# First attention of a fused attention and feed-forward kernel: the stride of the token order moved from a VectorE write to TensorE's transposes, and one row of weight rounding moved to the next stage

## The chip, the cores and the metric

The kernel runs on one core of a Trainium2 chip. The metric is the device time of one execution in microseconds. The kernel before took 1344.98 us (median of three runs, 1344.81 to 1346.94).

In the text PE is TensorE (PEld its weight loads), DVE is VectorE, ACT is ScalarE, POOL is GpSimd and SP is SyncE, whose queue issues nearly all transfers.

## What is computed

```python
# q, k, v: (8, 12, 448, 64) float32; g_q, g_k: (64,)
q_n, k_n = rmsnorm(q, g_q), rmsnorm(k, g_k)         # x / sqrt(mean(x*x) + 1e-6) * g, over the 64
scores = q_n @ k_n.T / sqrt(64)
attn = softmax(scores)                              # (448, 448) for each of 96 heads
attn_out = attn @ v
x = attn_out.transpose(0, 2, 1, 3).reshape(3584, 768)
h = x @ w_in                                        # (768, 2048), float64 weights
out = maximum(h, 0) ** 2 @ w_out                    # (2048, 768), float64 weights
```

## The kernel before

The eight batches are worked on in four spans of two batches. A span has an attention, a first product (`x @ w_in` and the squared ReLU) and a second product. Two heads make a pair, so that 128 partitions are filled, and a span has 12 pairs. The two products are done with seven smaller products each (named A11, S2, S1, S3, A12, A22, S4) in place of eight; this needs sums of weight blocks and of `x`.

Only the first span's attention runs with no product of an earlier span beside it: `attention_alone`. It and the first product after it, here called L1, are the stages that the change touches. On the trace the first runs until 133 us, L1 until about 262 us.

**The first attention.** A load of q puts four neighbouring tokens into one partition: partition p holds tokens 4p to 4p+3 (112 partitions). After the norm, `transpose(i, s, n)` turns each of the four chunks of q (s = 0) and of k (s = 1) with PE into a PSUM bank `pt` (L782), and ACT copies the bank to `qkT` (L784 for k, L786 for q with the gains). Chunk j has the tokens 4p+j, so the 448 columns of `qkT` stand in the order (j, p) and not in that of the tokens. Keys stand on partitions of the scores and may have any order, as long as v has the same. Queries are columns of the scores, of the values `pav` and of the sums `tot`, and stay in the order (j, p) until the end of the pair. There `finish(i)` makes the factors 1/sum with two DVE transposes and a reciprocal (L913 to L915), and multiplies (L922). This multiplication writes x in the order of tokens:

```python
            x = x.rearrange("d (p j) -> d j p", j=NJ)
            pav, factors = (t.rearrange("d (j p) -> d j p", j=NJ) for t in (pav, factors))
```

so that `pav` and `factors` are read one float after the other, and `xT` is written at every fourth float. `first_pair`, which runs ahead of the program's main part, has the same transposes for pair 0 (L380).

In a pair's turn stand, in this order: two score chunks and their exponentials (`scores`, L807 on PE, L811 on ACT), k's transposes for the next pair, the values' second half of the pair before (L870), the running sum of the exponentials (`add_up`, L824 on DVE), the norm's squares on ACT (L722) and their sums on DVE (L723, L724) for the pair after next, q's transposes for the next pair, the norm's root (`roots`, L733 to L738, on ACT, DVE and POOL), two more score chunks, the column sums `tot` (L895), the values' first half, and `finish` of the pair before. Each engine works through its own list in the order in which the code issues it; nothing is reordered by a scheduler.

**The rounding.** The weights come as float64, and are turned into float32 blocks on the chip in 32 rows, 16 of `w_in` and then 16 of `w_out`. `prepare(t)` is cut into four steps by its `yield`s; a row passes through a load of 768 KB (L540, L543), ACT (L589, L606), DVE (L603, L608, L613), and the sums of blocks on POOL (L583). For rows below `EARLY // 4` POOL also adds exponent and mantissa in two halves (`value`, L575); for later rows DVE does it in one instruction (L579). Every second row a store of seven blocks, 1344 KB, goes to DRAM (L598), from where PE's weights `sw` are read later (`load_blocks`, L672, five buffers). Loads, stores and `sw` are all in SP's queue.

How many steps stand beside which stage is set by two lines, one in the loop over `attention_alone` and one in that over L1 (u counts the turns; NAT is 12, N1 is 56, ALL is 140):

```python
    EARLY, ALL = 4 * 13, 4 * (2 * NFC + 3)
                weights(min(EARLY, 2 * u + 1, 4 + (EARLY - 4) * u // (4 * NAT - 7)))
                weights(min(ALL, EARLY + (ALL - EARLY) * (u - 1) // (N1 - 6)))
```

**L1.** For each of eight f there are seven groups of three matmul passes (L1098) against blocks `sw`; DVE adds their results (L1106, L1109, L1114), and ACT applies ReLU and square (L1066, L1068). The steps of the rounding stand between the groups.

Of the kernel before, what the change touches and what calls it, by code (L numbers as in the profile page):

```python
# [304 lines left out]
def places_of(qk, i, work):  # L305


    first, second = i % 2 * 4 + work, i % 2 * 4 + 2 + (i // 2 + work) % 2
    return qk[:, first:second + 1:second - first]


def load_q(nc, qk, q, i):

    _, H, S, D = q.shape
    b, h0 = divmod(2 * i, H)
    nc.sync.dma_start(places_of(qk, i, 0)[:S // 4, 0].rearrange("p (h e) -> p h e", h=2),
                      q[b, h0:h0 + 2].rearrange("h (p j) d -> p h (j d)", j=4))


def load_k(nc, qk, k, i):  # L320

    _, H, S, D = k.shape
    b, h0 = divmod(2 * i, H)
    dst = places_of(qk, i, 0)[:S // 4, 1].rearrange("p (j h d) -> p j h d", j=4, h=2)
    for h in range(2):
        nc.sync.dma_start(dst[:, :, h], k[b, h0 + h].rearrange("(p j) d -> p j d", j=4))


def normalise_in_turn(nc, raw, sq, rstd, mhalf, between=lambda: None):

    SP, _, n = rstd.shape
    for s in range(2):
        nc.scalar.activation(sq[:, s], raw[:, s], AF.Square)
        nc.vector.tensor_reduce(rstd[:, s], sq[:, s].rearrange("p (n d) -> p n d", n=n), AX, ALU.add)
        nc.vector.tensor_scalar(rstd[:, s], rstd[:, s], float(n) / sq.shape[2], 1e-6, ALU.mult, ALU.add)
        nc.gpsimd.tensor_tensor(rstd[:, s], rstd[:, s], mhalf[:SP, 0:n], ALU.pow)
        if s == 0:
            between()
            nc.vector.tensor_tensor(sq[:, 0].rearrange("p (j h d) -> p h j d", j=n // 2, h=2),
                                    raw[:, 0].rearrange("p (h j d) -> p h j d", j=n // 2, h=2),  # L340
                                    rstd[:, 0].rearrange("p (h j) -> p h j ()", h=2)
                                    .to_broadcast([SP, 2, n // 2, sq.shape[2] // n]), ALU.mult)


def first_pair(tc, q, k, g_q, g_k, held):

    nc = tc.nc
    qk, qkT, ident, mhalf, gains, rstd, bound = held
    D = q.shape[-1]
    S = q.shape[2]  # L350
    NJ = 4
    SP = S // NJ
    raw, sq = (places_of(qk, 0, n)[:SP] for n in range(2))
    load_q(nc, qk, q, 0)
    bound[0]()
    load_k(nc, qk, k, 0)
    for i, g in enumerate((g_q, g_k)):
        for h in range(2):
            nc.gpsimd.dma_start(gains[h * D:(h + 1) * D, i:i + 1], g.rearrange("(d o) -> d o", o=1))
    load_q(nc, qk, q, 1)  # L360
    load_k(nc, qk, k, 1)
    nc.gpsimd.memset(mhalf, -0.5)
    make_identity(nc, ident)


    def between():
        bound[1]()
        nc.vector.tensor_scalar(gains[:, 0:1], gains[:, 0:1], gains[:, 1:2], float(D) ** -0.5, ALU.mult, ALU.mult)

    with tc.tile_pool(name="ps_first", bufs=1, space=bass.MemoryType.PSUM) as ps_first:  # L370

        nc.vector.memset(qkT[:, 1], 0.0)
        idle = ps_first.tile([2 * D, S], F32, name="idle")
        for _ in range(3):
            nc.tensor.matmul(idle, qkT[:, 1, 0, 0:2 * D], qkT[:, 1, 1], start=True, stop=True)
        normalise_in_turn(nc, raw, sq, rstd, mhalf, between)
        for s, src in ((1, raw[:, 1]), (0, sq[:, 0])):
            pt = ps_first.tile([2 * D, S], F32, name=f"pt{s}")
            for j in range(NJ):
                nc.tensor.transpose(pt[:, j * SP:(j + 1) * SP], src[:, j * 2 * D:(j + 1) * 2 * D], ident[:SP, :SP])  # L380
            if s:
                nc.scalar.copy(qkT[:, 0, s], pt)
            else:
                nc.scalar.activation(qkT[:, 0, s], pt, AF.Copy, scale=gains[:, 0:1])
# [3 lines left out]
def attention_then_ffn_bounded(  # L388
# [35 lines left out]
    nc = tc.nc  # L424

    B, H, S, D = q.shape
    NT, DM = out.shape
    DFF = w_in.shape[1]
    P = 128
    NJ = 4  # L430
    SP = S // NJ
    NPAIR = H // 2
    NFC = DFF // P
# [26 lines left out]
    def bank(name, n=None):  # L460

        turn[0] += n is None
        return ps_m.tile([P, S], F32, tag="mn"[turn[0] % 2 if n is None else n], name=name)

    qk, qkT, ident, mhalf, gains, rstd0, _ = held
# [20 lines left out]
    HW = HC * P  # L486
    WORDS, BLOCKS, EXPS = 7, 2, 4

    EARLY, ALL = 4 * 13, 4 * (2 * NFC + 3)
    assert DM == NW and BLOCKS * 8 * HW + EXPS * NW + 2 * NW <= 3 * HF * S and 2 * NW <= 4 * S and HF % 4 == 0  # L490


# [184 lines left out]
    vs, probs, pavs, tots, normed, rstds = {}, {}, {}, {}, {}, {0: rstd0}  # L677
# [100 lines left out]
    def transpose(i, s, n):  # L778

        pt = bank("pt", n)  # L780
        for j in range(NJ):
            nc.tensor.transpose(pt[:, j * SP:(j + 1) * SP], normed[i][s][:, j * P:(j + 1) * P], ident[:SP, :SP])  # L782
        if s:
            nc.scalar.copy(qkT[:, i % 2, s], pt)  # L784
        else:
            nc.scalar.activation(qkT[:, i % 2, s], pt, AF.Copy, scale=gains[:, 0:1])  # L786
# [116 lines left out]
    def finish(i):  # L903

        b, hp = divmod(i, NPAIR)
        x = factors = xT[:, b % 2, hp]
        if i < NAT:
            pav = pavs.pop(i)


            turned, factors = sums["turned"], sums["factors"]
            few = small.tile([P, S // 32], F32, tag="few", name="few", bufs=1)
            nc.vector.transpose(turned, tots.pop(i))  # L913
            nc.vector.reciprocal(few, turned.rearrange("p (g r) -> p g r", r=32)[:, :, 0])
            nc.vector.transpose(factors.rearrange("p (g r) -> p g r", r=32),  # L915
                                few.rearrange("p g -> p g ()").to_broadcast([P, S // 32, 32]))

            x = x.rearrange("d (p j) -> d j p", j=NJ)
            pav, factors = (t.rearrange("d (j p) -> d j p", j=NJ) for t in (pav, factors))
        else:  # L920
            pav = rests.pop(i)
        nc.vector.tensor_tensor(x, pav, factors, ALU.mult)  # L922
        del vs[i]
# [15 lines left out]
    def attention_alone():  # L939


        for i in range(NAT):
# [5 lines left out]
            if i == 0:  # L948

                transpose(1, 1, 1)  # L950
                scores(0, 2)
                scores(0, 3)
                transpose(1, 0, 0)
                add_up(0, 1)
                norm(2)
                load_v(1)
                values(0, (0, 1))
                load(3)
                yield
                continue  # L960
            if more:
                transpose(i + 1, 1, 0)
# [16 lines left out]
            total_of(i - 1)  # L979
            values(i, (0, 1))  # L980
            finish(i - 1)
            yield
            if added(i) == 3:
# [5 lines left out]
        values(i, (2, 3))  # L989
        total_of(i)  # L990
        finish(i)
        combine_x(i)

    def attention(first):
# [3 lines left out]
        for i in range(first, last + 1):  # L998
# [42 lines left out]
            if i > first:  # L1041
                finish(i - 1)
                combine_x(i - 1)
# [511 lines left out]
def kernel(  # L1555
# [41 lines left out]
    with tc.manual_schedule():  # L1597

        nc.scalar.preload_act_table_set("natural_log_exp_and_others")
        first_pair(tc, q, k, g_q, g_k, held)  # L1600
# [4 lines left out]
    with tc.If(bits <= limit) as small_scores:  # L1605
        with tc.manual_schedule():
            attention_then_ffn_bounded(tc, *args, held)
# [32 lines left out]
```

## Time and profile before

| | before |
|---|---|
| median of three runs | 1344.98 us |
| the profiled execution | 1345.02 us |
| its span | 1343.1 us |
| granted PE clock | 0.998 |
| PE busy, share of the span | 1324.0 us, 99% |
| DVE busy | 860.5 us, 64% |
| ACT busy | 486.2 us, 36% |
| POOL busy | 681.1 us, 51% |
| first matmul of L1 starts at | 133.3 us |

Busy time of an engine is the time that its instructions took, and a share is an average over stages with different limits. A matmul's recorded time overlaps with the next one's, so a group of matmuls is read by its length from first start to last end. The difference of 1.9 us between the execution and its span lies around the program. In the answers below, "A <- B" after an idle time names the instruction that ended it.

### The profile page before, as it was taken

The numbers are of one execution on the slowest core, as the hardware profiler recorded it, in microseconds if no ns is written. First come the engines' busy times: TensorE is split into PE (matmuls) and PEld (weight loads), VectorE is DVE, ScalarE is ACT, GpSimd is POOL, SyncE is SP. The second block draws the span as 40 slices with busy tenths as digits, with TensorE's granted clock in tenths as the row PEclk, the third lists the DMA queues.
The fourth block names the chain that finished last, engine by engine and source line by source line (L and its number), as shares of the span: only waits on it lengthen the run. The fifth ranks groups of instructions, "written<-read, shape, count | busy, mean of one in ns | idle before, by whom it ended". The sixth has DMA issues, their size and how long they took to land.

```text
span 1343.1 us, 17769 instructions
## 1 busy us (share of the span) xinstructions
PE 1324.0 (99%) x5930; PEld 699.4 (52%) x5930; DVE 860.5 (64%) x1333; ACT 486.2 (36%) x939; POOL 681.1 (51%) x546
## 2 busy tenths in 40 slices
PE   8999999999999999999999999999999999999997
PEld 3333544444446655444444755444444665556887
DVE  6999888489988233467887523457878723336553
ACT  7886566455541012245543011235554101111000
POOL 5766534376765222647774522448676522322452
PEclk9999999999999999999999999999999999999999
DMA  8978899656664433356656432345664444431333
GB/s 225 240 221 218 289 372 307 213 124 132 133 148 119 102 88 88 97 116 125 145 127 144 109 91 88 95 114 115 134 130 124 120 92 143 128 88 47 115 104 55
DMA packets 413817, 190.18 MB, mean 142 GB/s; under 512 B 282388, under 2 KB 408724, under 8 KB 413716
## 3 DMA queue, kind: packets, MB, share of 16 engines
q1 hardware_dynamic: 406164, 180.21, 51.8%
q0 software_dynamic: 4736, 8.40, 2.4%
q8 instruction: 49, 0.80, 0.3%
q10 hardware_dynamic: 2816, 0.34, 0.2%
q14 instruction: 52, 0.43, 0.1%
HBM read 155.72 MB, written 33.16 MB: 141 GB/s over the span
## 4 chain that ended last, share of the span: by engine, by line
PE 86%; DVE 7%; ACT 3%; DMA 3%; issue 1%; POOL 0%; SPq 0%; DVEq 0%; ACTq 0%; POOLq 0%
PE ps L1198 21%; PE pd L1098 10%; PE pa L1098 10%; PE pc L1098 10%; PE sc L799 7%; PE pav L881 7%; PE pb L1098 5%; PE ps L1381 3%; PE ps L1249 2%; PE pd L1353 2%; PE pc L1353 2%; PE pa L1353 2%; PE pd L1183 1%; PE pc L1183 1%; DMA sw<-w1s 1%
## 5 line engine op out<-in xcount | busy, mean ns | idle before, releaser
L1070 POOL TENSOR_TENSOR gT<-gT 128x448 f32<-128x448 f32 x96 | 93.7, 978 | 258.5 <-ACT gT L1066 258.5
L764 POOL TENSOR_TENSOR half<-half,mhalf 128x28 f32<-128x28 f32 x36 | 185.2, 5145 | 69.5 <-DVE half L763 54.9
L1198 PE MATMUL ps<-gT,sw 128*128 128x448 f32 x432 | 169.3, 545 | 0.0
L1066 ACT ACTIVATE gT<-gT 128x448 f32<-128x448 f32 x96 | 55.4, 577 | 296.2 <-DVE gT L1114 296.2
L1098 PE MATMUL pa<-xT,sw 128*128 128x448 f32 x384 | 154.9, 539 | 0.5 <-DMA sw<-w1s 0.5
L1198 PEld LDWEIGHTS ps<-gT,sw 128*128 128x128 f32 x432 | 80.1, 190 | 87.2 <-issue 85.0
L1198 PE MATMUL ps<-gC,sw 128*128 128x448 f32 x288 | 113.1, 546 | 0.0
L799 PE MATMUL sc<-qkT 64*64 64x448 f32 (+1 forms) x1152 | 110.0, 496 | 0.3 <-ACT pr L801 0.2
L1098 PEld LDWEIGHTS pa<-xT,sw 128*128 128x128 f32 x384 | 72.8, 190 | 71.4 <-issue 71.4
L583 POOL TENSOR_TENSOR gC<-gC 128x384 f32<-128x384 f32 x64 | 76.3, 1209 | 60.2 <-DVE gC L579 58.5
L1114 DVE TENSOR_TENSOR gT<-z,pd 128x448 f32<-128x448 f32 x32 | 19.8, 620 | 102.2 <-PE pd L1098 102.2
L849 POOL DMA_DIRECT2D xT<-factors x72 | 38.0, 532 | 92.8 <-DMA factors<-square 65.7
L1198 PEld LDWEIGHTS ps<-gC,sw 128*128 128x128 f32 x288 | 53.2, 190 | 59.5 <-issue 58.3
L801 ACT ACTIVATE pr<-sc 128x896 f32<-128x896 f32 x87 | 76.9, 908 | 12.3 <-PE sc L799 12.1
L766 POOL TENSOR_TENSOR qk<-qk,half 128x448 f32<-128x448 f32 x72 | 77.1, 1092 | 2.8
L1098 PE MATMUL pd<-xT,sw 128*128 128x448 f32 x192 | 77.9, 542 | 0.2
L1098 PE MATMUL pc<-xT,sw 128*128 128x448 f32 x192 | 77.5, 540 | 0.2 <-DMA sw<-w1s 0.2
L1098 PE MATMUL pd<-xC,sw 128*128 128x448 f32 x192 | 77.4, 539 | 0.0
L1098 PE MATMUL pb<-xC,sw 128*128 128x448 f32 x192 | 77.4, 539 | 0.0
L1098 PE MATMUL pc<-xC,sw 128*128 128x448 f32 x192 | 77.4, 539 | 0.0
L881 PE MATMUL pav<-pr,vt 64*64 64x448 f32 x348 | 72.7, 537 | 0.0
L881 PE MATMUL rest<-pr,vt 64*64 64x448 f32 x348 | 72.7, 537 | 0.0
(282 smaller groups left out, 2453.1 us busy)
## 6 DMA issues: line engine op xcount, KB each, us to landing
sw<-w1s SPq DMA_DIRECT2D x224, 192.0 KB, 2.4
sw<-w2s SPq DMA_DIRECT2D x102, 256.0 KB, 3.4
w1s<-gC SPq DMA_DIRECT2D x8, 1344.0 KB, 6.4
w2s<-gC SPq DMA_DIRECT2D x8, 1344.0 KB, 6.8
qk<-in_q_dram SPq DMA_DIRECT2D x144, 56.0 KB, 2.6
qk<-in_k_dram SPq DMA_DIRECT2D x144, 56.0 KB, 2.4
xT<-factors POOLq DMA_DIRECT2D x72, 112.0 KB, 3.5
words<-in_moe_w_out_dram SPq DMA_DIRECT2D x9, 768.0 KB, 6.9
```

The costliest lines, as they stand in the source:

```text
L583: nc.gpsimd.tensor_tensor(*[blocks_of(n)[:, place_of(n, i)] for i in (dst, x, y)], op)
L764: nc.gpsimd.tensor_tensor(half, half, mhalf, ALU.pow)
L766: nc.gpsimd.tensor_tensor(qkn[:, s], raw[:, s], half[:, s * NG:(s + 1) * NG].rearrange("p g -> p g ()").to_broadcast([P, NG, 32]), ALU.mult)
L799: nc.tensor.matmul(sc[part, h, 0:n], qkT[rows, 0, 1, keys], qkT[rows, 0, 0, of], start=True, stop=True)
L801: nc.scalar.activation(pr, sc[:, :, 0:n], AF.Exp)
L881: nc.tensor.matmul(into, vs[i][rows, h, c, :], probs[i, c][rows, h, :], start=(c == 0), stop=(c == NF), skip_group_check=True)
L1066: nc.scalar.activation(g, src, AF.Relu)
L1070: nc.gpsimd.tensor_tensor(g, g, g, ALU.mult)
L1098: nc.tensor.matmul(ps, stream[n + at][:, c], rhs[:, c], start=first and c == 0, stop=c == HC - 1, skip_group_check=not first)
L1198: nc.tensor.matmul(ps, stream[n][:, c % 4], rhs_of[i][:, c], start=c == 0, stop=c == HF - 1)
L1353: nc.tensor.matmul(ps, lhs[:, c], rhs[:, c], start=first and c == 0, stop=c == HK - 1, skip_group_check=not first)
L1381: nc.tensor.matmul(ps, weights_of(o, m, c // HK)[:, c % HK], rhs_of[i][:, c, part], start=c == 0, stop=c == HF - 1)
```

## The change

Three things change, all in the first span. q's transposes (s = 0) write chunk j to the columns j, j+4, j+8 and so on of the bank, so that the columns come in the order of tokens from there on; k's transposes (s = 1) write as before. The multiplication in `finish` then reads and writes everything in that order, with no rearrangement. And `EARLY` is 48 in place of 52, so that twelve rows of the rounding lie beside the attention and twenty beside L1; row 12 is then one of those whose exponent and mantissa DVE adds.

```diff
+def chunk_of(pt, s, j, n):
+
+    return pt.rearrange("d (j p) -> d j p", j=n)[:, j] if s else pt.rearrange("d (p j) -> d j p", j=n)[:, j]
+
+
 def first_pair(tc, q, k, g_q, g_k, held):
...
-                nc.tensor.transpose(pt[:, j * SP:(j + 1) * SP], src[:, j * 2 * D:(j + 1) * 2 * D], ident[:SP, :SP])
+                nc.tensor.transpose(chunk_of(pt, s, j, NJ), src[:, j * 2 * D:(j + 1) * 2 * D], ident[:SP, :SP])
...
-    EARLY, ALL = 4 * 13, 4 * (2 * NFC + 3)
+    EARLY, ALL = 4 * 12, 4 * (2 * NFC + 3)
...
-            nc.tensor.transpose(pt[:, j * SP:(j + 1) * SP], normed[i][s][:, j * P:(j + 1) * P], ident[:SP, :SP])
+            nc.tensor.transpose(chunk_of(pt, s, j, NJ), normed[i][s][:, j * P:(j + 1) * P], ident[:SP, :SP])
...
-
-            x = x.rearrange("d (p j) -> d j p", j=NJ)
-            pav, factors = (t.rearrange("d (j p) -> d j p", j=NJ) for t in (pav, factors))
```

## The prediction

> **What bounds the kernel now.** I first asked where the time is made, with the windows view over the two stages that the change touches: the first attention, until 133 us, and the first product L1, until 262 us. The columns are the stretch, its length, busy time (and instructions) of PE, PEld, DVE, ACT and POOL, then clock, DMA share, GB/s.
>
> ```profile
> 31.00:107.00 76.00, 71.70 (x368) 27.31 (x370) 72.95 (x105) 61.83 (x112) 50.19 (x39) 1.00 0.81 231
> 107.00:133.00 26.00, 25.47 (x128) 9.76 (x124) 23.91 (x36) 17.95 (x34) 18.75 (x10) 1.00 0.88 216
> 133.00:240.00 107.00, 106.28 (x281) 53.06 (x281) 92.16 (x116) 60.32 (x93) 48.21 (x46) 1.00 0.93 324
> ```
>
> From 31 to 107 us PE (71.70 of 76) and DVE (72.95 of 76) are both nearly full; DVE is at 96%. In L1 PE is full, DVE is at 86%, the DMA engines at 93%. Which of the two ends last in the attention is told by the chain of work that ended last (start, length, what):
>
> ```profile
> 31.21 1.07 DVE gT L824
> 32.28 1.14 DVE rstd L723
> ...
> 37.89 0.66 DVE gT L915
> 38.57 1.03 DVE xT L922
> ...
> 40.31 1.89 DVE gT L824
> 42.20 1.14 DVE rstd L723
> ...
> 47.17 0.99 DVE xT L922
> ...
> 114.44 1.69 PE sc L807 x8
> ```
>
> It runs mostly through DVE until 107 us, with the multiplication of `finish` (L922) in it, and is PE alone from 114 us on. What PE loses by it is in its waits up to 265 us (total us, times, longest):
>
> ```profile
> PE pt L782 <- ACT qkT L784: 3.2, 7, 1.0
> PE sc L807 <- ACT gT L811: 2.2, 3, 1.0
> PE pa L1098 <- DMA sw<-w1s: 0.5, 1, 0.5
> ```
>
> ACT is only the messenger: in the same stretch its own longest wait is for DVE (L733 for the sums of L724: 13.9 us in 8 waits). So the attention can give back a few microseconds of PE's idle time, no more.
>
> [...] where every operand is contiguous and one is in PSUM (L1106: 618 ns), and L922, which writes every fourth float, takes 997 ns. [...] the trace's excess is (997-618)/448 = 0.85 ns an element. [...] Nothing in this trace has PE writing with a stride[...].
>
> ```profile
> L922 DVE TENSOR_TENSOR xT<-pav,gT 128x448 f32<-128x448 f32 x12 | 12.0, 997 | 0.4
> L1106 DVE TENSOR_TENSOR z<-p,pb 128x448 f32<-128x448 f32 x11 | 6.8, 618 | 19.9 <-PE pb L1098 18.4 <-ACT gC L589 1.4
> 38.39 0.60 PE L782 MATMUL pt<-ident,qk 112*128 112x112 f32 x4
> ```
>
> **The change, part by part.** (1) `finish`: 12 multiplications lose the stride. 12 x (0.997-0.618) = 4.5 us of DVE. Seven of them lie between 31 and 107 us, where DVE sets the pace: 2.7 us there. No wait is added or removed.
>
> (2) Row 12 of the rounding goes from the attention to L1. The attention runs 44 steps instead of 48 over the same 41 turns, so DVE loses one each of L603, L608 and L613 (0.8+0.95+0.95 = 2.7 us), ACT one L606 and one L589 (0.92 each, 1.8 us), POOL about two adds L575 (1.1 to 1.4 us each), and SP's queue one load of 768 KB and one store of 1344 KB. Spread evenly, 76/125 of DVE's 2.7 us, 1.6 us, falls between 31 and 107.
>
> Together DVE has 2.7 + 1.6 = 4.3 us less to do there: 68.7 us against PE's 71.7. DVE is then no longer the fuller engine, and PE is late next. What PE can win is its own slack: the idle stretches in its timeline from 31 to 107 us are 1.02, 0.80, 0.21, 0.43, 1.02, 0.17, 0.98 and 0.22, 4.9 us, and the three score runs behind such a gap last 2.05 instead of 1.76 us, 0.9 us more. So the gain lies between 0 and 5.8 us, and not above 4.3 where DVE is the cause, plus up to 0.5 us of gaps after 107. The chain also holds ACT's exponentials, POOL's scaling L738 and loads of k (one of 5.05 us at 57.4), which the change doesn't shorten. I take **3.5 us**, between 1.5 and 5.
>
> (3) q's 48 transposes write with a stride. Four take 0.60 us, of which the last one's own 0.26 us is latency: (0.60-0.26)/3 = 0.113 us from start to start. A 448-column matmul of L1 is issued every 2.25/6 = 0.375 us, 0.84 ns a column, so 112 columns at that rate take 94 ns: a transpose has about 20 ns to spare, and its pace is probably that of its weight load (140 ns of its own row, overlapping). [...] I take **no cost**, hidden under the weight load. If PSUM charges what SBUF charges (0.85 ns x 112 = 95 ns each), PE gets 48 x 0.095 = 4.6 us more, nearly all in a stage where PE is at 94%. A gain is excluded: nothing is taken away. ACT's copies L784 and L786 read `pt` as before.
>
> (4) L1 takes what the attention gives. DVE there: 2.7 us plus the add of row 12, which it now does itself (L579, 1.0 to 1.1 us): 3.8 us. DVE waits for PE's outputs in all about 26 us of L1's 129 us and so has room on average, but the steps come denser: 92 instead of 88 over the same 50 turns, 4.5% more. Where DVE is fullest (9.58 of 10 us from 180 to 190) it gets to 9.9, and PE's banks are freed later behind it; there before already one matmul group lasted 2.52 instead of 2.25 us. DMA: 2.1 MB more on 39.5 MB. From 150 to 210 us the engines are at share 1.0 and 365 to 404 GB/s; 2.1 MB at 375 GB/s are 5.6 us, of which the nearly idle start (136 GB/s from 130 to 140) takes a part. SP's queue carries rows, stores and the blocks `sw` in one order. A store waits for POOL's sums (L583; 6.9 us in 6 waits), and with it each `sw` behind it, for which PE waits:
>
> ```profile
> 217.68 8.72 DMA sw<-w1s
> 226.44 2.52 PE pc L1098 x6
> ...
> 232.16 6.18 DMA sw<-w1s
> 238.48 2.49 PE pa L1098 x6
> ```
>
> Five buffers of `sw` are 11.3 us of PE's work, landing takes 4.6 us in the middle and 8.7 at most; most of the addition is covered by that lead. I take **1.0 us** lost, between 0 and 3 (a block landing late by the whole 5.6 us less part of the lead).
>
> Sum: -3.5 + 0 + 1.0 = **-2.5 us**. The stages after 262 us keep their order and are PE's. The profiled execution took 1345.02 us (span 1343.1 and 1.9 around it), beside a median of 1344.98, so both give the same: **1342.5 us**.
>
> **The rivals.** *A: the strided write is dear* (slower). Its place is L782, its price from 0.095 us each upward. At 0.095, 4.6 us of PE eat the 3.5 gained: -3.5+4.6+1.0 = +2.1, 1347 us. At twice that, 0.19 us, 9.1-3.5+1.0 = +6.6: 1351.6. It decides from (3.5-1.0)/48 = 52 ns a transpose on (a spacing of 165 ns instead of 113), and is seen as slower from 5.2/48 = 108 ns. [...] against it the slow column rate of these float32 passes and the weight load beside them.
>
> *B: L1 gives all back.* DMA and DVE there are near full at once; a stall like those at 226 and 238 us, repeated in five or six places at 0.5 to 0.8 us, makes 3 to 4 us: 1345 to 1346. For it the share of 1.0, against it PE's total of less than 1 us of idle time there now.
>
> *C: everything is hidden in L1 and the attention reaches PE's pace:* -4 to -5 us, 1340.5. For it DVE's 4.3 us; against it the chain's other members.
>
> **How the numbers follow.** 0.2%, 2.7 us, is about what a measurement of this kernel can tell from no change. The likeliest case (0.55) runs from -4.5 to 0 with -2.5 in its middle: 0.30 faster, 0.25 same. C (0.10) is faster. B (0.15): 0.09 same, 0.06 slower. A (0.20): 0.06 same, 0.14 slower. Sums: faster 0.40, same 0.40, slower 0.20. The likeliest case alone spans 1340.5 to 1345. The range takes in most of C and of B, and A until somewhat under twice SBUF's price: 1339.8 to 1349.
>
> **What would show it.** Right: L922's successor near 620 ns; four transposes of q still 0.57 to 0.60 us; PE's waits at L782 and L807 down from 5.4 us to under 2.5; the first matmul of L1 at about 129.8 us instead of 133.3; L1 at 129 to 131 us, its waits for `sw` about 1 us. Wrong: four transposes of q lasting 0.9 us or more (A); the first L1 matmul earlier but L1's end not, with longer waits for `sw` or for DVE's reads of PSUM (B); DVE faster and PE's gaps unchanged, which would say that loads of k or ACT hold the chain.

## The result, and the profile after

The changed kernel takes **1341.43 us** (median of 13 runs, 1339.04 to 1344.22), the kernel before 1344.03 us (median of 13 runs on the same chip, 1343.54 to 1346.94). By the medians it is 2.6 us faster. The ratio, estimated over all these runs, is 0.9973, with a 95% interval from 0.9966 to 0.998: 3.6 us faster, between 2.7 and 4.6. The profiled execution took 1340.13 us (span 1338.3), which is 4.9 us less than the profiled one of before and 1.3 us under its own median; the executions after the change scatter over 5 us, those of before over 3.

The windows of the kernel after, with the columns as before. The first is the same stretch; the others end where L1 now begins and where the profile of before was cut, three microseconds earlier.

```profile
31.00:107.00 76.00, 74.87 (x386) 28.66 (x388) 70.10 (x110) 63.90 (x116) 52.28 (x41) 1.00 0.81 232
107.00:130.00 23.00, 22.77 (x113) 8.80 (x112) 19.24 (x30) 14.34 (x27) 14.94 (x8) 1.00 0.65 170
130.00:237.00 107.00, 105.00 (x279) 52.45 (x278) 94.52 (x116) 62.62 (x96) 49.54 (x46) 1.00 0.96 342
```

From 31 to 107 us PE is busy for 74.87 us instead of 71.70, and has 386 matmul records instead of 368: more work of the attention fits into the same time. DVE has 2.85 us less. In L1 DVE and the DMA engines are fuller than before, and PE is less full (105.00 instead of 106.28 of 107 us).

The chain of work that ended last, after the change (start, length, what), first in the attention, then in L1:

```profile
31.51 1.69 PE sc L812 x8
33.20 1.65 PE tot L900 x8
...
36.35 1.69 PE sc L812 x8
...
38.58 1.65 PE pav L875 x8
...
40.77 1.69 PE sc L812 x8
...
49.88 1.91 DVE gT L829
...
89.65 1.90 DVE gT L829
99.46 1.89 DVE gT L829
...
204.65 7.98 DMA sw<-w1s
212.67 2.52 PE pc L1100 x6
...
228.43 6.18 DMA sw<-w1s
234.75 2.49 PE pa L1100 x6
```

Where DVE's `add_up` and sums stood at 31, 32, 40 and 42 us, PE's scores, sums and values stand now. The chain has not left DVE: from 45 to 53 us and from 84 to 104 us it still runs through it. With its short pieces counted, DVE has 25.2 us of the chain between 31 and 107 us instead of 52.3, and PE 37.9 us instead of none. The two blocks `sw` on which L1 hung before are there still. The waits of PE up to 265 us (total us, times, longest) and DVE's multiplication among the costliest groups:

```profile
PE pt L787 <- ACT qkT L789: 2.0, 5, 1.0
PE pa L1100 <- DMA sw<-w1s: 1.5, 1, 1.5
...
PE sc L812 <- ACT gT L816: 0.6, 1, 0.6
PE pc L1100 <- DMA sw<-w1s: 0.5, 1, 0.5
```

```profile
L924 DVE TENSOR_TENSOR xT<-pav,gT 128x448 f32<-128x448 f32 x11 | 6.9, 625 | 0.4
```

The timeline of PE shows q's transposes and the start of L1:

```profile
40.17 0.60 PE L787 MATMUL pt<-ident,qk 112*128 112x112 f32 x4
...
128.28 2.52 PE L1100 MATMUL pa<-xT,sw 128*128 128x448 f32 x6
```

PE's waits at the transposes and scores fell from 5.4 to 2.6 us, and those for `sw` rose from 0.65 (0.50 and 0.15) to 2.0 us. L1 starts at 128.28 us (before 133.23 us) and ends at 257.47 us (before 261.20).

Not all of the 5.0 us at L1's start belong to the change. The multiplication of the first `finish`, early in the attention, already starts 0.45 us sooner:

```profile
27.55 0.99 DVE L922 TENSOR_TENSOR xT<-pav,gT 128x448 f32<-128x448 f32 x1
27.10 0.63 DVE L924 TENSOR_TENSOR xT<-pav,gT 128x448 f32<-128x448 f32 x1
```

The first line is of before, the second of after. This start lies between 26.7 and 28.1 us in the profiles below, and it scatters where the programs do not differ: in e5 and e7, which have the instructions of before up to there, it is 28.05 and 27.98 us. Counted from this multiplication, L1 begins after 101.2 us instead of 105.7: **4.5 us won in the attention, and 1.2 us given back in L1 in this execution**. The last 32 matmuls start at 1324.70 instead of 1328.38 us, 3.7 us earlier. The other 1.1 us of this execution's gain lie after them, and I don't count them for the change.

### The profile page after: what moved, and what is told of

It is laid out like the page before. It is cut to its first block, busy times and chain, and to the rows that moved or that the text cites. A ratio compares the mean times of both kernels' runs of the same rounds, so it can differ in the third digit from the quotient of the medians.

```text
span 1338.3 us, 17760 instructions
## 1 busy us (share of the span) xinstructions
PE 1322.2 (99%) x5930; PEld 698.8 (52%) x5930; DVE 857.3 (64%) x1334; ACT 486.5 (36%) x939; POOL 681.2 (51%) x544
## 4 chain that ended last, share of the span: by engine, by line
PE 91%; DVE 3%; ACT 3%; DMA 1%; issue 1%; POOL 0%; SPq 0%; ACTq 0%; DVEq 0%
PE ps L1200 21%; PE pd L1100 10%; PE pa L1100 10%; PE pc L1100 10%; PE sc L804 7%; PE pav L886 7%; PE pb L1100 5%; PE ps L1383 3%; PE ps L1251 2%; PE pd L1355 2%; PE pc L1355 2%; PE pa L1355 2%; PE sc L812 1%; PE pd L1185 1%; PE tot L900 1%; PE pc L1185 1%
## 5 line engine op out<-in xcount | busy, mean ns | idle before, releaser
L588 POOL TENSOR_TENSOR gC<-gC 128x384 f32<-128x384 f32 x64 | 71.6, 1136 | 62.4 <-DVE gC L584 60.7
```

The lines of the kernel that those rows point to most:

```text
L588: nc.gpsimd.tensor_tensor(*[blocks_of(n)[:, place_of(n, i)] for i in (dst, x, y)], op)
```

## The experiments

Two questions were open: which part of the change gave the attention's gain, and why it was more than the 3.5 us expected; and what L1's loss is made of. One measure is used throughout, from DVE's timeline: the **stretch** from the start of `finish`'s multiplication (L922 before, L924 after) to the start of the norm's sums (L723, L728) in the same pair's turn. It is on the loop that sets the attention's pace: exponentials, `add_up`, sums, root, next exponentials, next scores. Seven of them lie between 31 and 107 us. Since the start of the attention scatters, "L1 from first" counts L1's start from the start of the first `finish`'s multiplication.

| kernel | median us (runs) | ratio to before, 95% interval | L1 starts | L1 from first | L1 lasts | seven stretches |
|---|---|---|---|---|---|---|
| before | 1344.03 (13) | | 133.23 | 105.7 | 128.0 | 36.4 |
| after | 1341.43 (13) | 0.9966 to 0.998 | 128.28 | 101.2 | 129.2 | 33.2 |
| e1 stride alone | 1344.8 (13) | 0.9992 to 1.0008 | 132.72 | 105.7 | 128.3 | 36.2 |
| e2 row alone | 1342.47 (22) | 0.9979 to 0.9992 | 129.77 | 103.0 | 128.0 | 34.5 |
| e3 after, again | 1340.19 (5) | 0.9948 to 0.9974 | 128.34 | 101.5 | 130.4 | 33.1 |
| e4 after, q, k and v loaded early | 1344.32 (13) | 0.9985 to 1.0001 | 128.43 | 101.6 | 132.8 | 33.2 |
| e5 before, no sums beside | 1340.87 (6) | 0.9956 to 0.998 | 129.87 | 101.8 | 128.0 | 32.0 |
| e6 stride alone, no sums beside | 1340.91 (6) | 0.9958 to 0.9982 | 129.44 | 101.4 | 128.0 | 31.7 |
| e7 row alone, old places | 1343.86 (21) | 0.999 to 1.0003 | 132.58 | 104.6 | 128.5 | 36.5 |
| e8 after, q transposed twice | 1343.05 (17) | 0.9978 to 0.9992 | 131.38 | 103.4 | 128.3 | 33.2 |
| e9 stride and 13 rows, new places | 1341.77 (18) | 0.9974 to 0.9989 | 127.98 | 101.2 | 129.6 | 33.2 |
| e10 after, strided products | 1340.4 (8) | 0.9958 to 0.9979 | 127.98 | 101.2 | 128.0 | 33.2 |
| e11 after, q, k and v loaded later | 1338.33 (5) | 0.9942 to 0.9969 | 127.95 | 101.2 | 127.2 | 33.2 |
| e12 stride alone, no adds beside | 1339.52 (6) | 0.9953 to 0.9978 | 128.21 | 101.5 | 128.0 | 31.6 |

Kernels e1 to e4, e5 to e8 and e9 to e11 ran together, on one chip each, with runs of the kernel before, which the ratios refer to (about 1344 to 1345 us everywhere); e12 ran by itself beside before.

**e1: the stride alone.** The kernel after with thirteen rows beside the attention.

```diff
-    EARLY, ALL = 4 * 12, 4 * (2 * NFC + 3)
+    EARLY, ALL = 4 * 13, 4 * (2 * NFC + 3)
```

> The changed kernel with EARLY back at 4 * 13: only q's strided transposes and the multiplication in token order are changed. Theory D (VectorE's time set the pace of the first attention; the stride took 4.5 us of it, the row 2.7 us): the first matmul of L1 starts about 3 us earlier than before (133.3 us), L1 stays 128 us long, total -2.5 to -3.5 us against before. Rival R (the row does it, through fewer transfers and fewer GpSimd adds beside VectorE; the stride is hidden): the first matmul of L1 moves by less than 1 us, total within 1 us of before. The transposes: four in 0.60 us in both theories; 0.9 us or more would show that the strided write is dear and only covered.

Measured: 1344.8 us, ratio 1.0. L1 starts 0.5 us earlier, but counted from the first multiplication not at all (105.7 us in both); PE's gaps are those of before. DVE's multiplication takes 0.62 us as it should, and its busy time from 31 to 107 us falls, but only by half of 2.7 us:

```profile
31.00:107.00 76.00, 72.17 (x370) 27.54 (x372) 71.60 (x104) 61.95 (x113) 50.02 (x39) 1.00 0.84 232
```

Where the rest goes is seen by laying the timelines of DVE and POOL of both kernels side by side at one pair (start, length). Before:

```profile
78.07 1.97 POOL L583 TENSOR_TENSOR gC<-gC 128x384 f32<-128x384 f32 x2
78.76 1.01 DVE L922 TENSOR_TENSOR xT<-pav,gT 128x448 f32<-128x448 f32 x1
79.59 2.83 DVE L608 TENSOR_SCALAR gC<-gC 128x768 uint32<-128x768 uint32 x1
80.01 1.99 POOL L575 TENSOR_TENSOR gC<-words,gC 128x384 int32<-128x384 int32 x2
82.45 0.96 DVE L613 SCALAR_TENSOR_TENSOR gC<-gC 128x768 uint32<-128x768 uint32 x1
```

With the stride's change alone:

```profile
77.59 1.97 POOL L588 TENSOR_TENSOR gC<-gC 128x384 f32<-128x384 f32 x2
78.28 0.62 DVE L924 TENSOR_TENSOR xT<-pav,gT 128x448 f32<-128x448 f32 x1
78.82 3.11 DVE L613 TENSOR_SCALAR gC<-gC 128x768 uint32<-128x768 uint32 x1
79.52 1.98 POOL L580 TENSOR_TENSOR gC<-words,gC 128x384 int32<-128x384 int32 x2
81.96 0.96 DVE L618 SCALAR_TENSOR_TENSOR gC<-gC 128x768 uint32<-128x768 uint32 x1
```

The next instruction of DVE (which takes 0.55 us at 43.10 us with the stride alone, where POOL is idle from 40.90 to 44.64 us) starts 0.3 us sooner behind the multiplication and lasts 0.28 us longer. It ends 0.4 us after POOL's adds in both kernels. From the multiplication's start to that of the third line on DVE it is 3.69 us before and 3.68 us here: the multiplication is shorter and nothing else begins earlier. Over all seven stretches 36.4 became 36.2 us, although seven times 0.37 us were saved. So beside POOL's sums and adds a DVE instruction lasts 2.83 and 3.11 us in place of 0.55, and all of it is recorded as busy time, with no wait before it. What in the chip ties the two engines together, these traces don't show.

**e2: the row alone.** The kernel before with twelve rows.

```diff
-    EARLY, ALL = 4 * 13, 4 * (2 * NFC + 3)
+    EARLY, ALL = 4 * 12, 4 * (2 * NFC + 3)
```

> The kernel before with EARLY at 4 * 12 and nothing else. Theory D: the row's 2.7 us of VectorE bring the start of L1 forward by about 2 us, L1 gets 1 to 1.5 us longer, total -0.5 to -1 us. Rival R: the start of L1 comes 4 us or more earlier, nearly all of the changed kernel's 5.0, total -2.5 us.

Measured: 1342.47 us, ratio 0.9986. L1 starts 3.5 us earlier; counted from the first multiplication it is 2.7 us, as much as the DVE work that leaves. From 31 to 107 us:

```profile
31.00:107.00 76.00, 73.79 (x382) 28.04 (x380) 70.05 (x108) 62.47 (x114) 49.57 (x39) 1.00 0.82 226
```

L1 lasts as long as before, with 1.1 us of waiting for `sw`. So in this execution the row's own loads and stores are not much of a burden there. Of the two parts, taken alone, the row is the one that brings something. The chain agrees: from 31 to 107 us it has no PE in it in e1, and 40.3 us of PE here.

**e3: the changed kernel again,** beside e1, e2 and e4.

> The changed kernel once more, as the measure for the runs beside it: about -2.6 us against before (both theories), start of L1 at 128 to 129 us, L1 129 to 130 us.

Measured: 1340.19 us, ratio 0.9961. L1 starts within 0.1 us of the first profile's time, but lasts 130.4 instead of 129.2 us, with waits for `sw` of 0.79 us at 154, 0.32 us, and 1.68 us at 236 us. The attention is the same in both profiles of this kernel; L1's waits are what scatters.

**e4: the next span's loads earlier.** In L1, twelve DMA issues in SP's queue load q, k and v for the next span, at turn 40. They stand ahead of the `sw` blocks that come late. Here they are issued at turn 2.

```diff
-                if u == 5 * N1 // 7:
+                if u == 2:
```

> The changed kernel with the loads of v and of q and k for the next attention issued at turn 2 of L1 in place of turn 40. Theory Q (what L1 gives back, 1.3 us in the trace, is waiting for weight blocks that stand in SP's queue behind these 12 transfers while the engines are full): the two waits of 0.48 and 1.52 us fall below 0.5 us in all, L1 is 127.5 us long, total 1 to 2 us below the changed kernel. Rival S (the waits come from the sum of bytes, or from stores waiting for GpSimd): they stay at 1.5 to 2 us or move to other groups, total within 0.7 us of the changed kernel.

Measured: 1344.32 us, ratio 0.9993: everything lost. The late waits are nearly gone, but new ones of 0.40, 0.46 and 2.50 us stand near the start, and the group behind the longest runs slowly too. PE's timeline:

```profile
157.53 3.98 PE L1100 MATMUL pa<-xT,sw 128*128 128x448 f32 x6 [2.50 <-DMA sw<-w1s]
...
218.13 2.52 PE L1100 MATMUL pc<-xC,sw 128*128 128x448 f32 x6 [0.26 <-DMA sw<-w1s]
```

The issues occupy SP's queue from 134 to 142 us, just where the lead of five blocks is being built up. The loads do move the wait, but this place is worse. L1 lasts 132.8 us.

**e5 and e6: no sums of POOL beside the attention.** Both leave out POOL's sums (L583, L588) for the rows 5, 7, 9 and 11; e5 is the kernel before with this, e6 the stride alone (e1) with it. The theory tested, P, is that in lines like those of e1 DVE, though recorded as busy, waits for POOL, and that this hides the stride's gain; its rival O says that the order of each engine's list does.

```diff
-            if there(n) and n % 2:
+            if there(n) and n % 2 and not 4 < n < 12:
```

> The kernel before, leaving out GpSimd's sums of weight blocks for rows 5, 7, 9 and 11 of the rounding (16 of the 24 sums that stand beside the first attention; the blocks keep old values, so later products use wrong weights). It is the base for e6. Theory P ([...] a part of VectorE's busy time in the first attention is such waiting): VectorE's busy time from 31 to 107 us falls by 3 us or more though it has the same work, and L1 starts 2 us or more before 133.2 us. Theory O (the order of ACT's and VectorE's lists alone makes the gaps): busy time and start of L1 within 1 us of before.

> e5 with the strided transposes and the multiplication in token order (EARLY 4 * 13), leaving out the same sums. Theory P [...]: without GpSimd in the way the stride's part shows, L1 starts 1.5 us or more earlier than in e5, total 1.5 us or more below e5. Theory O: no more than in e1, 0.5 us.

Measured: 1340.87 and 1340.91 us. Without the sums DVE is busy for 70.80 us from 31 to 107 us in e5 (before 72.95), 2.15 us less, though six more of its instructions lie in this stretch; 3 us or more were expected:

```profile
31.00:107.00 76.00, 73.10 (x380) 28.24 (x380) 70.80 (x111) 65.56 (x119) 39.42 (x33) 1.00 0.91 252
```

L1 starts 3.4 us earlier (3.9 from the first multiplication). So the sums do cost DVE time. But the stride brings no more than in e1: e6 starts L1 0.43 us before e5, and its seven stretches are 0.3 us shorter. The second half of P, as tested here, fell. These two kernels kept POOL's *other* instruction beside `finish`, the adds of exponent and mantissa (L575, L580), to which DVE's ends are tied in the lines of e1; e12 takes that up.

**e7: the row without its places.** The pace of the rounding is `EARLY - 4` steps over 41 turns: 48 before, 44 after. One row fewer thus moves every later step to another turn. Here there is one row fewer, but the steps stay in their turns of before until row 12 is due. Theory T says that the places count.

```diff
-                weights(min(EARLY, 2 * u + 1, 4 + (EARLY - 4) * u // (4 * NAT - 7)))
+                weights(min(EARLY, 2 * u + 1, 4 + 48 * u // (4 * NAT - 7)))
```

> e2 (12 rows beside the attention, strided multiplication as before) with the steps of these rows at the pace of before, 48 steps over 41 turns until 48 are done, so that the first 36 turns have exactly the instructions of before in their order. Theory A (the amount: less work for VectorE): the gain comes with the missing row, L1 starts at about 131 to 132 us. Theory T (the places of the steps in the turns): L1 starts within 1 us of before's 133.2 us, against 129.8 in e2, and the gaps of PE at 57, 77, 82 and 99 us are there as before.

Measured: 1343.86 us, ratio 0.9997. L1 starts at 132.58 us, 0.65 us earlier than before, and 1.1 us counted from the first multiplication. PE's timeline has the gaps of before again:

```profile
57.30 2.06 PE L807 MATMUL sc<-qkT 64*112 64x448 f32 x8 [0.81 <-ACT gT L811]
...
77.82 2.06 PE L807 MATMUL sc<-qkT 64*112 64x448 f32 x8 [0.40 <-ACT gT L811]
...
83.07 0.57 PE L782 MATMUL pt<-ident,qk 112*128 112x112 f32 x4 [1.01 <-ACT qkT L784]
...
99.71 2.06 PE L807 MATMUL sc<-qkT 64*112 64x448 f32 x8 [0.98 <-ACT gT L811]
```

So a row taken from the end of the attention is worth about 1.1 us; the rest of e2's 2.7 us comes with the slower pace ahead of it.

**e9: the places without the row.** The counterpart: thirteen rows as in e1, at the pace of twelve.

```diff
-                weights(min(EARLY, 2 * u + 1, 4 + (EARLY - 4) * u // (4 * NAT - 7)))
+                weights(min(EARLY, 2 * u + 1, 4 + 44 * u // (4 * NAT - 7)))
```

> e1 (strided transposes, multiplication in token order, 13 rows) with the rounding's steps at the changed kernel's pace, 44 over 41 turns; the steps of row 12 then stand in the last turns of the attention, after 110 us, where PE alone sets the end. Only the places of the steps differ from e1, which had L1 start at 132.7 us. Theory T (places): L1 starts at 128.5 to 130 us, total 3 us or more below e1, and L1 loses less than in the changed kernel, so the total is at or below the changed kernel's. Theory A (amount): L1 starts within 1 us of e1's 132.7 us, total as before.

Measured: 1341.77 us, ratio 0.9982. L1 starts at 127.98 us, 4.7 us earlier than in e1 (4.5 from the first multiplication), with the same instructions in another order. From there it is as early as in the kernel after, from which the row's work is gone altogether. Its stretches are those of the kernel after to a few hundredths (4.84, 5.16, 3.53, 4.45, 3.99, 5.76 and 5.48 us). Before they were 3.55, 5.74, 5.22, 6.15, 5.57, 6.20 and 3.95. In four of the seven of before two of DVE's rounding instructions stand within the stretch; in the new places only in the last two. The slower pace also thins the middle: from the first multiplication of `finish` to the ninth DVE has 26 instructions of the rounding here, as in e2 and after, and 29 before and in e1 and e7; behind it, until L1, there are nine here and six before. So e9 does not tell the new places of the steps from a whole row's fewer in the middle. A step carries pieces of ACT, POOL and SP too, which move with it. L1 has 1.20 and 1.06 us of waiting for `sw` here and lasts 129.6 us, against 129.2 after.

**e8: is a strided transpose dear?** q's transposes are issued twice, k's are not.

```diff
-            nc.tensor.transpose(chunk_of(pt, s, j, NJ), normed[i][s][:, j * P:(j + 1) * P], ident[:SP, :SP])
+            for _ in range(1 if s else 2):
+                nc.tensor.transpose(chunk_of(pt, s, j, NJ), normed[i][s][:, j * P:(j + 1) * P], ident[:SP, :SP])
```

> The changed kernel with each of q's transposes in the attention's loop issued twice to the same columns: 44 more strided transposes, 44 x 0.113 = 5.0 us of PE. If PE is what the attention now waits for, L1 starts 4 to 5 us later than in the changed kernel (128.3 us) and the total rises by as much; if there is still slack it rises by 2 us or less. It gives the price that a dear strided write would have had.

Measured: 1343.05 us, ratio 0.9985. PE's timeline:

```profile
31.88 0.96 PE L788 MATMUL pt<-ident,qk 112*128 112x112 f32 x8 [0.54 <-ACT qkT L790]
```

Eight take 0.96 us where four take 0.57 to 0.60: 0.09 to 0.10 us for one more. That is at or below the 0.113 us from start to start of contiguous ones, so a strided write has no excess. The 44 added transposes are about 4.3 us; L1 starts 3.1 us later than after the change, of which 0.8 us were there already at the first multiplication, so 2.3 us are left. The rest of the 4.3 fell into PE's remaining gaps: its waits in the attention went down from 2.6 to 1.0 us.

**e10: a stride in the large products.** The same question for 448 columns. L1's products and those of the later spans write PSUM at every fourth float. As written, `x` is still read one float after the other, so the columns come out in another order than that of the tokens, and the read at a stride that the expectation below speaks of is not there.

```diff
-                    nc.tensor.matmul(ps, stream[n + at][:, c], rhs[:, c], start=first and c == 0,
+                    nc.tensor.matmul(ps.rearrange("d (p j) -> d j p", j=4), stream[n + at][:, c], rhs[:, c].rearrange("d (j p) -> d j p", j=4), start=first and c == 0,
```

> The changed kernel with all 1344 matmuls of the four first products (448 columns, three to six accumulated in one bank) writing their PSUM columns in the order (j, p) with a stride of four floats, x's columns read in that order; the columns, and so the result, are the same. It asks for the price of a strided PSUM write where PE is the bound. If a stride costs nothing at these float32 passes: six passes in 2.25 us as now, total within 1 us of the changed kernel. If PSUM charges 0.85 ns an element as SBUF charged VectorE: six passes in 4.5 us, total higher by 500 us. The read of x with a stride of 112 floats has its own risk: if it costs, the passes get longer too and the two can't be told apart.

Measured: 1340.4 us, ratio 0.9969. The group of L1's first product, of this kernel from 128 to 260 us (x count, busy us, mean ns, idle before):

```profile
L1100 PE MATMUL pa<-xT,sw 128*128 128x448 f32 x96 | 38.9, 541 | 1.0 <-DMA sw<-w1s 1.0
```

and of the kernel after:

```profile
L1100 PE MATMUL pa<-xT,sw 128*128 128x448 f32 x96 | 38.9, 541 | 1.5 <-DMA sw<-w1s 1.5
```

541 ns in both, and six of them in 2.25 us in both. The price that rival A carried over to PE, the 0.85 ns an element of DVE's strided write in the trace of before, doesn't hold for PE's write of float32 at a stride of 16 bytes in this kernel.

**e11: the next span's loads in two parts.** e4 had shown the loads' weight and a wrong place. Here the loads of q and k are issued at turn 44 and those of v at turn 48, in place of all at 40.

```diff
-                if u == 5 * N1 // 7:
-                    load_v(NAT)
+                if u == 44:
                     load(NAT + 2)
+                if u == 48:
+                    load_v(NAT)
```

> The changed kernel with the loads for the next attention in L1 split and moved later: q and k at turn 44, v at turn 48 in place of both at turn 40, when the rounding's own loads are over. Theory Q (sw waits behind the 12 issues in SP's queue while the engines are full): PE's wait near 235 us (1.5 us) falls under 0.5 us, L1 about 128 us long, total 1 us or more below the changed kernel. Rival S: the wait moves to 240 to 250 us with the loads, total within 0.5 us of the changed kernel.

Measured: 1338.33 us, ratio 0.9955: the fastest of all kernels here, 6.1 us under before on its chip. One wait for `sw` is left in L1:

```profile
212.11 2.52 PE L1100 MATMUL pc<-xC,sw 128*128 128x448 f32 x6 [0.24 <-DMA sw<-w1s]
```

L1 lasts 127.2 us, where PE's own 56 groups at 2.255 us make 126.3 us. So PE's waits in L1 are mostly for blocks that stand behind these loads in SP's queue; before, where L1 lasts 128.0 us, has a part of them too. The kernel after didn't run beside e11, but e10 did, which times like it: 1340.4 us (1339.27 to 1340.89) against 1338.33 (1337.21 to 1339.57).

**e12: no adds of POOL.** The stride alone (e1), without POOL's adds (L580) for rows 5 to 11; its sums stay.

```diff
-            if not there(n):
+            if not there(n) or 4 < n < 12:
                 return
```

> The stride alone (13 rows beside the attention), with POOL's adds of exponent and mantissa (L580) left out for rows 5 to 11; POOL's sums (L588) stay, so the result is not the reference's in these rows. In the stride-only kernel the rounding instruction of DVE behind finish's multiplication (L924) takes 1.26, 1.18, 3.11 and 1.58 us in four pairs, where the same instruction alone takes 0.55 to 0.95, and it ends 0.8 to 1.5 us after POOL's add ends; the seven stretches from L924 to the sums L728 between 31 and 107 us are 36.23 us together, against 36.38 before the change, although L924 saves 0.37 us in each. Theory P (the saving is spent in waiting for POOL's adds, so they, and not the sums left out earlier, are what hides it): without the adds these instructions take 0.55 to 0.95 us in every pair, the seven stretches together fall below 33.5, and the first matmul of L1 starts at 128.5 to 130.5 us instead of 132.7. Theory O (the saving is lost in the order of the lists, to loads and to ACT's exponentials, whatever POOL does): the instructions may get shorter, but waits for ACT or for loads at add_up and L728 take their place; the seven stretches stay above 35 us and L1 starts at 132 us or later.

Measured: 1339.52 us, ratio 0.9966. The stretches fall to 31.6 us and L1 starts at 128.21 us, somewhat beyond what P expected. The 3.11 us instruction is down to 1.17 us (not 0.95 or less: one of POOL's sums stands beside it):

```profile
77.10 0.62 DVE L924 TENSOR_TENSOR xT<-pav,gT 128x448 f32<-128x448 f32 x1
77.65 1.17 DVE L613 TENSOR_SCALAR gC<-gC 128x768 uint32<-128x768 uint32 x1
78.85 0.96 DVE L618 SCALAR_TENSOR_TENSOR gC<-gC 128x768 uint32<-128x768 uint32 x1
80.30 1.09 DVE L829 TENSOR_TENSOR gT<-gT 112x896 f32<-112x896 f32 x1 [0.49 <-ACT gT L816]
81.74 1.22 DVE L728 TENSOR_REDUCE rstd<-qk 112x16 f32<-112x1024 f32 x1 [0.34 <-ACT qk L727]
```

Counted from the first multiplication, the adds are therefore worth some 4.2 us of L1's start to the kernel with the stride. What they are worth without it was not run, so the stride's share in these 4.2 us is not known. And O has a part: the last four stretches are 5.31, 4.64, 4.42 and 2.88 us, those of e6 5.35, 4.64, 4.43 and 2.88, those of e5 5.35, 4.64, 4.42 and 3.08, and e5 still has the slow multiplication. Three kernels with different work come to the same lengths. With these instructions of POOL out of the way DVE waits for ACT's exponentials and squares, as the two brackets show, and the saved 0.37 us goes into that wait.

## Why the prediction was right, and where a step failed

**The sum.** Predicted was -3.5 in the attention, nothing for the transposes, +1.0 in L1: -2.5 us. The attention gave 4.5 us and the transposes cost nothing. L1 lasted 1.2 us longer than before in the first profile and 2.4 us longer in e3's, but only 0.3 us in e8's and no longer in e10's, which have the same rows beside it and the same transfers. The medians differ by 2.6 us, which meets the forecast almost exactly. But the ratio says 2.7 to 4.6 us, and 3.5 to 7.0 us in e3, so the true gain is probably larger, and the close match is in part luck.

**The transposes.** Right. Four take 0.60 us with the stride, and e8 and e10 show that neither a transpose nor a product pays for it. Rival A needs 52 ns each; nothing near it is there. The reason given, that the write hides under the weight load of 140 ns, is not shown: in e8 one more transpose, with its weight load, takes under 0.1 us, and e10's products, 375 ns apart beside weight loads of 190 ns, have no such cover and pay nothing either. A's sum was also too harsh: e8 did add 44 times 98 ns to PE, nearly its lower price, and was still 1.5 us faster than before by the medians, because PE's gaps took a part.

**Which engine is late next.** Right in part: PE took the place of half of DVE's share in the chain (37.9 us, DVE 25.2 instead of 52.3), PE's waits at L787 and L812 fell to 2.6 us (under 2.5 was given), and more work for PE then cost time (e8). L924 takes 625 ns, where near 620 was expected.

**The attention's 3.5 us: the step that failed.** "Together DVE has 2.7 + 1.6 = 4.3 us less to do there" added DVE's microseconds as if all were worth the same. For both parts together this comes near the 4.5 us measured, nearer than the 3.5 us that were taken; for each part it does not hold. Counted from the first multiplication, the stride's 2.7 us brought nothing alone (e1) and 1.8 us on top of the row (4.5 less e2's 2.7). The row brought 2.7 us alone, and 1.1 us when it was taken from the attention's end (e7). Nor did it leave evenly: at the pace of 44 steps over 41 turns three of DVE's rounding instructions, a whole row's, leave the middle, and it makes no difference whether they are then done in the last turns (e9) or beside L1 (after): 101.2 us in both. So a microsecond of DVE has no price of its own; it depends on where the instruction stands. A reading that fits, argued from the stretches and not shown: a rounding instruction within a stretch delays the sums, the root, the next exponentials and the next scores, and one outside can hide under a wait.

That DVE was busy for 96% of the time was also misread. A part of that busy time comes from POOL's work beside it: leaving out POOL's sums took 2.15 us off DVE's busy time, with six instructions more in the stretch (e5). And DVE does not pass on all that it is relieved of while POOL's adds stand beside it: seven times 0.37 us were saved in e1, and the seven stretches became 0.2 us shorter.

**L1.** Its +1.0 was near the first profile's 1.2, small for e3 and too much for e8 and e10. Its mechanism (`sw` late in SP's queue behind other issues) is shown by e4 and e11. But it isn't the row's own DMA, which the step priced at 5.6 us of the engines' time: e2 has the row there and loses nothing. It is mostly the loads of q, k and v for the next span. Why these blocks come later in the kernel after than in e2, with the same rows in L1, was not separated; the scatter between profiles, up to 2.4 us, is larger than that difference. Rival B, with 3 to 4 us given back, is approached only by e3's 2.4; rival C's time was met by the first profile (1340.1) although L1 did not hide all there; in e10 (1340.4) it did, so C was a nearer guess than its chance says. PE's pace, which C asked for, was not reached: DVE still has its 25.2 us of the chain.

**Still open:** how the gain of the slower pace divides between a row's fewer instructions in the middle, POOL's work beside DVE and the order of DVE's list. e12 with e5 and e6 shows that the last two are there; a kernel with the places of before and no POOL work beside it at all was not tried. Nor was the new pace with thirteen rows and without the stride, which would say how much of e9's 4.5 us needs the stride.

## What to carry to other kernels

Price a relief of a busy engine in the stretch between two of its hand-overs, not by its busy time: follow what comes next in its list, and ask whether that was held up by something else (here by POOL's adds and by ACT's exponentials). When a loop's count sets the pace at which other work is mixed in, changing the count moves every later piece; moving a piece to the end of a stage can be worth as much as taking it away (e9). And when a stage gives back time at a queue, look for the block of issues ahead of the late transfer and try more than one place for it, since the first one may be worse.

## What the runs showed of the hardware

Writes of PE into PSUM at every fourth float32 cost nothing that can be seen: 541 ns a product of 448 columns with and without the stride, and 0.60 us for four transposes of 112. DVE's write to SBUF at the same stride costs 0.83 ns an element (997 against 625 ns for 448). And a DVE instruction of 0.55 us is recorded with up to 3.11 us beside POOL's sums and adds, all of it as busy time and none as a wait.
